# Normalised attention followed by a squared-ReLU network: the last row tile's seven products in another order, its upper rows stored by halves, and the weight pieces converted at other due times

## The chip, the cores and the metric

The kernel runs on one core of a Trainium2 chip. The metric is the device time of one execution in microseconds (us), lower being better. Four executions of the kernel before gave a median of 1434.13 us, from 1432.71 to 1435.56. The profile is of one execution that took 1433.29 us, of which the profiled span is 1431.9 us.

## The reference

There are 8 batches, 12 heads, 448 rows and a head width of 64. Queries and keys are normalised by their root mean square and multiplied by a gain; softmax attention follows; its output, with the heads side by side, is a matrix of 3584 rows by 768. Two matrix products with a squared ReLU between them follow.

```python
q_n, k_n = rmsnorm(q, g_q), rmsnorm(k, g_k)
attn = softmax(q_n @ k_n.T / sqrt(64))
x = (attn @ v).transpose(0, 2, 1, 3).reshape(3584, 768)
h = maximum(x @ w_in, 0.0)          # w_in: 768 x 2048
out = (h * h) @ w_out               # w_out: 2048 x 768
```

All activations are 32-bit floats. The two weight matrices come as 64-bit floats, because the reference multiplies them by a 64-bit scalar; the kernel turns their bits into 32-bit floats itself.

## The kernel before, in words

**Four passes.** The network runs in four passes `ffn(u)`, u = 0 to 3, of two batches each. Both products are done with seven block products P1 to P7 in place of eight, so each matrix is kept as quarters and as sums of quarters: `IN` and `OUT` list the forms of a piece of `w_in` and `w_out` (the tiles `in_sb` and `out_sb`), and `make_x_forms` and `hidden_sum` make the forms of the left factors. The attention of the first two batches stands ahead of pass 0; the attention of later batches is woven into passes 0, 1 and 2. Pass 3 has no attention beside it.

**One block.** A pass has four blocks. In a block, `first_products` (L696) runs twice, seven products of three steps of the inner dimension each (L705); ACT copies four of the product banks to SBUF (L712), DVE adds a bank and a copy to give the hidden values (L725), ACT does the ReLU and the square (L726, L727). Then `second_products` (L743) does the rows left over (L757), and for three row tiles `tt` the seven products of `SECOND_ORDER` (L786). After each product DVE adds the PSUM bank to the accumulator tile (`add_to`, L827; L803 where it subtracts). `upper_acc` holds c11 and c12 as its two halves of 384 columns, `lower_acc` holds c21 and c22. Three PSUM banks play the three roles in turn: role 0 takes P1, P6 and P7 one upon another, role 1 takes P5 and P3, role 2 takes P2 and then P4. So P6 may not start before c11's addition of P1 has read the bank, P4 not before that of P2, P7 not before that of P6.

**The last block of a pass stores.** When a row tile's accumulator is complete, `(tt, 0)` (upper) and `(tt, 1)` (lower) go into `to_store`, and at P2, at P4 and at the end of the block all that wait there are stored, on SP's queue, as whole rows of 768 (L832). In `SECOND_ORDER` P3 completes c12 and P7 completes c21 and c22, so the last store of the kernel is that of the lower rows of tile 2, after P7 and two additions.

**Steps and their cost.** Each generator step ends in a `yield` of a cost: 18 for a product of `first_products`, 15, 15, 5, 5 for the rows left over, 10 for a product of the row tiles. A block's sum is 14 x 18 + 40 + 21 x 10 = 502, a pass's 2008. `run(until)` takes steps until the cost spent reaches a mark; between marks the attention's instructions are emitted (a "visit", every 2008 / 24 = 83.7, and the turning of the next pair's queries or keys halfway between visits). After every step `run` emits one `make_sum` (L942), one `end_join` (L911), whatever conversions are due, and a few of the attention's small tasks. The order of emission is the order on each engine.

**Conversion of the weights.** There are 64 pieces: for each block eight of `w_in` and eight of `w_out`, each 128 x 384 numbers of 64 bits (384 KB). The call `convert()` number n does four things:

- it ends the open join and begins that of piece n-1 (`join_words`, DVE, L900; the end, at the latest one step on, is two more DVE instructions, L920 and L924);
- it asks SP to load piece n+2 (L868, L873); there are three `words` buffers, so this load waits until the join of piece n-1 has ended, and SP's later loads stand behind it;
- it splits piece n on ACT (three activations, L887 to L889), for which that piece must have landed;
- after the fourth piece of a tile, four sums of forms follow, one a step, on DVE and POOL in turn (L946), and a store of the tile to DRAM (L948), from which passes 1 to 3 load the forms again.

The first 17 calls are made while the attention runs alone (`early`). The other 48 are made within pass 0, when the cost spent reaches the next entry of `late`. Before, entry j stands at 502 + 2 + 31.375 (j - 8): sixteen to a block, evenly. The pieces of `w_in` for the next block fall in the second half of a block, those of `w_out` in the first half of the block that uses them.

Of the kernel before, what the change touches and what calls it, by code (L numbers as in the profile page):

```python
# [21 lines left out]
P = 128  # L22
# [201 lines left out]
def program(ctx, tc, rows, v, g, wide, ones, moe_w_in, moe_w_out, out, shift):  # L224

    nc = tc.nc

    B, H, S, D = v.shape
# [5 lines left out]
    HALF = DM // 2  # L234
    REST = S % P
    NT = S // P
    NBLK = 4
# [431 lines left out]

    FIRST_ORDER = ["P1", "P5", "P2", "P6", "P3", "P4", "P7"]  # L670
    SECOND_ORDER = ["P1", "P2", "P5", "P6", "P4", "P3", "P7"]
    COST_IN, COST_OUT = 12 * NK // 2, 10
    COST = NF // 2 * 7 * COST_IN + NBLK * (NT * 7 + 4) * COST_OUT

# [68 lines left out]
    def second_products(u, blk, hid, sums_, accs):  # L743

        flat = [a.rearrange("p t e s -> p t (e s)") for a in hid]
        ns = [u * NF // 2 + 2 * blk + t for t in range(2)]
        w_sb = [out_sb[n] for n in ns]
        s1, s2, s4 = sums_
        for n in range(4):
            hidden_sum(hid, sums_, 1, n)  # L750

        parts = [(0, 0), (1, 0), (0, 1), (1, 1)]
        for some in (parts[:3], parts[3:]):
            for half in range(2):
                ps = roles[half][:, 0:HALF]
                for a, t in some:
                    nc.tensor.matmul(  # L757
                        ps, lhsT=flat[a][:, t, ds(NT * P, P)], rhs=w_sb[t][:, 2 * a + half, :],
                        start=(a, t) == parts[0], stop=(a, t) == parts[-1],
                    )  # L760
                if some[-1] == parts[-1]:
                    add_to(accs[-1][:, ts(half, HALF)], ps, blk == 0)
                yield len(some) * COST_OUT // 2
        turn_roles(2, 1, 0)

        def store_rows(tt, e):
            queues = (nc.sync, nc.scalar if final and (tt, e) == (NT - 1, 1) else nc.sync)
            if tt is None:
                parts = [(2 * u, P * NT, REST), (2 * u + 1, 0, REST)]
            else:  # L770
                parts = [(2 * u + e, REST * e + P * tt, P)]
            store(accs[-1 if tt is None else 2 * tt + e], parts, queues)

        to_store = deque([(None, 0)])
        final = u == B // 2 - 1
        (a11, s3), (a12, a22) = [(a[:, :, LOWER], a[:, :, UPPER]) for a in flat]
        lefts = {"11": a11, "12": a12, "22": a22, "S1": s1, "S2": s2, "S3": s3, "S4": s4}
        for tt in range(NT):
            upper_acc, lower_acc = accs[2 * tt], accs[2 * tt + 1]
            c11, c12 = [upper_acc[:, ts(h, HALF)] for h in range(2)]  # L780
            c21, c22 = [lower_acc[:, ts(h, HALF)] for h in range(2)]
            for name in SECOND_ORDER:
                role, first, left, right = PRODUCTS[name]
                ps = roles[role][:, 0:HALF]
                for t in range(2):
                    nc.tensor.matmul(  # L786
                        ps, lhsT=lefts[left][:, t, ts(tt, P)], rhs=w_sb[t][:, OUT.index(right), :],
                        start=first and t == 0, stop=t == 1,
                        skip_group_check=not first,
                    )  # L790
                if name == "P1":
                    add_to(c11, ps, blk == 0)
                elif name == "P5":
                    add_to(c22, ps, blk == 0)
                elif name == "P2":
                    add_to(c11, ps)
                elif name == "P6":
                    add_to(c12, ps, blk == 0)
                elif name == "P4":
                    if blk == 0:  # L800
                        nc.scalar.mul(c21, ps, -1.0)
                    else:
                        nc.vector.tensor_tensor(out=c21, in0=c21, in1=ps, op=ALU.subtract)  # L803
                elif name == "P3":
                    add_to(c12, ps)
                else:
                    add_to(c21, ps)
                    add_to(c22, ps)
                    to_store.append((tt, 1))
                if name == "P3":  # L810
                    to_store.append((tt, 0))
                if name in ("P2", "P4") and blk == NBLK - 1:
                    while to_store:
                        store_rows(*to_store.popleft())
                yield COST_OUT
            turn_roles(2, 0, 1)
        while to_store and blk == NBLK - 1:
            store_rows(*to_store.popleft())
        for n in ns:
            del out_sb[n]  # L820
            load_out(n + 2)
# [130 lines left out]
    def convert():  # L952
# [13 lines left out]
    block, tile_pieces = COST // NBLK, 4  # L966
    ahead = 4 * tile_pieces
    early = deque(2 + 2.4 * n for n in range(ahead + 1))
    every = block / ahead
    late = deque(  # L970
        block + 2 + every * (n - 2 * tile_pieces) for n in range(len(all_pieces) - ahead)
    )

    load_weights(0)
    load_weights(1)
# [273 lines left out]
```

## Time and profile before

| | |
|---|---|
| median of 4 runs | 1434.13 us |
| profiled execution, its span | 1433.29 us, 1431.9 us |
| PE, DVE, ACT, POOL busy | 1407.1, 659.8, 592.9, 676.5 us |
| attention alone | 0 to 135.7 us |
| pass 0, blocks 0 to 3 | from 135.7, 227.1, 319.7 and 409.1 to 501.2 us |
| last block of pass 3 | 1360.9 to 1424.8 us |

PE is the matrix engine, PEld its weight loads, DVE the vector engine, ACT the scalar engine, POOL the general engine, SP the engine whose queue (SPq) starts nearly all DMAs. In a timeline row come the start and the busy time in us, the engine, the line of the kernel, the operation, what it writes and reads, how many instructions are merged, and in brackets the idle time before it and what ended it. In a row of waits come the waiting engine and line, what it waited for, the total in us, how often, and the longest.

### The profile page before, as it was taken

The numbers are of one execution on the slowest core, as the hardware profiler recorded it, in microseconds if no ns is written. First come the engines' busy times: TensorE is split into PE (matmuls) and PEld (weight loads), VectorE is DVE, ScalarE is ACT, GpSimd is POOL, SyncE is SP. The second block draws the span as 40 slices with busy tenths as digits, with TensorE's granted clock in tenths as the row PEclk, the third lists the DMA queues.
The fourth block names the chain that finished last, engine by engine and source line by source line (L and its number), as shares of the span: only waits on it lengthen the run. The fifth ranks groups of instructions, "written<-read, shape, count | busy, mean of one in ns | idle before, by whom it ended". The sixth has DMA issues, their size and how long they took to land.

```text
span 1431.9 us, 15428 instructions
## 1 busy us (share of the span) xinstructions
PE 1407.1 (98%) x4932; PEld 681.8 (48%) x4932; DVE 659.8 (46%) x1233; ACT 592.9 (41%) x1114; POOL 676.5 (47%) x676
## 2 busy tenths in 40 slices
PE   7999999999999999999999999999999999999997
PEld 3333444444444445445454544445454455555554
DVE  5997366877768523324252452324233241132413
ACT  6874566557555244442425234351432303212130
POOL 5667654746656646446445565464462422011110
PEclk9999999999999999999999999999999999999999
DMA  5765346664676664444435464343622242313122
GB/s 141 194 194 154 66 112 176 167 204 141 197 203 200 193 174 98 150 112 127 117 68 173 113 182 128 98 133 76 180 70 89 94 154 78 116 50 127 38 89 80
DMA packets 309279, 188.12 MB, mean 131 GB/s; under 512 B 265796, under 2 KB 293316, under 8 KB 300996
## 3 DMA queue, kind: packets, MB, share of 16 engines
q1 hardware_dynamic: 308896, 186.97, 44.8%
q8 instruction: 41, 0.67, 0.2%
q14 instruction: 50, 0.41, 0.1%
q10 hardware_dynamic: 292, 0.07, 0.0%
HBM read 144.57 MB, written 42.40 MB: 131 GB/s over the span
## 4 chain that ended last, share of the span: by engine, by line
PE 89%; DVE 4%; SPq 1%; DMA 1%; issue 1%; POOL 1%; ACT 1%; DVEq 0%; POOLq 0%; ACTq 0%
PE bank L705 35%; PE bank L786 29%; PE bank L477 9%; PE bank L397 8%; PE bank L757 5%; PE bank L507 1%; PE bank L516 1%; PE bank L490 1%; DVE acc L827 1%; SPq L157 1%; PE bank L362 0%; DVE out_sb L946 0%; DMA q_rows<-qk 0%; SPq L166 0%; DVE out_sb L924 0%
## 5 line engine op out<-in xcount | busy, mean ns | idle before, releaser
L705 PE MATMUL bank<-xT,in_sb 128*128 128x448 f32 x1344 | 515.4, 542 | 0.0
L705 PEld LDWEIGHTS bank<-xT,in_sb 128*128 128x128 f32 x1344 | 252.4, 190 | 260.4 <-issue 250.7
L827 DVE TENSOR_TENSOR acc<-acc,bank 128x384 f32<-128x384 f32 x324 | 173.7, 549 | 233.0 <-PE bank L786 185.0
L786 PE MATMUL bank<-out_sb,hid 128*128 128x384 f32 x768 | 266.6, 487 | 0.5 <-DVE acc L827 0.5
L725 DVE TENSOR_TENSOR hid<-bank,part 128x448 f32<-128x448 f32 x128 | 76.9, 621 | 329.3 <-PE bank L705 329.0
L405 ACT ACTIVATE wT<-bank,rr 128x448 f32<-128x448 f32 x288 | 161.2, 633 | 121.5 <-PE bank L397 70.5
L786 PE MATMUL bank<-out_sb,sums 128*128 128x384 f32 x576 | 203.8, 490 | 2.7 <-DVE acc L827 2.6
L786 PEld LDWEIGHTS bank<-out_sb,hid 128*128 128x128 f32 x768 | 145.4, 190 | 104.5 <-DVE acc L827 2.4
L202 POOL TENSOR_TENSOR rr<-ms,minus_half 128x8 f32<-128x8 f32 (+1 forms) x96 | 146.4, 1525 | 92.8 <-DVE ms L195 81.8
L741 POOL TENSOR_TENSOR sums<-hid 128x384 f32<-128x384 f32 x32 | 32.3, 1008 | 301.9 <-ACT hid L727 301.9
L397 PE MATMUL bank<-qT,kT 64*128 64x448 f32 (+1 forms) x768 | 164.4, 573 | 1.5 <-DVE qT L370 1.1
L726 ACT ACTIVATE hid<-hid 128x448 f32<-128x448 f32 x128 | 73.3, 572 | 196.8 <-DVE hid L725 196.8
L786 PEld LDWEIGHTS bank<-out_sb,sums 128*128 128x128 f32 x576 | 107.7, 190 | 87.1 <-issue 8.1
L712 ACT COPY part<-bank 128x448 f32<-128x448 f32 x128 | 67.8, 529 | 175.4 <-PE bank L705 175.4
L424 POOL TENSOR_TENSOR sum<-sum,wT 128x448 f32<-128x448 f32 (+1 forms) x96 | 110.4, 1171 | 10.8 <-ACT wT L405 8.1
L397 PEld LDWEIGHTS bank<-qT,kT 64*128 64x128 f32 (+1 forms) x768 | 55.6, 173 | 103.9 <-issue 69.1
L477 PE MATMUL bank<-wT,vt 128*64 128x448 f32 x480 | 102.2, 546 | 0.0
L757 PE MATMUL bank<-out_sb,hid 128*128 128x384 f32 x256 | 85.6, 488 | 0.0
L528 POOL COPY few<-few 32x14 f32<-32x14 f32 x48 | 9.1, 189 | 153.3 <-DVE few L526 151.4
L424 POOL TENSOR_TENSOR sum<-wT 128x448 f32<-128x448 f32 x48 | 57.1, 1209 | 50.4 <-ACT wT L405 50.4
L192 DVE TENSOR_REDUCE ms<-squares 128x8 f32<-128x512 f32 (+1 forms) x68 | 41.8, 614 | 77.0 <-ACT squares L179 77.0
L727 ACT ACTIVATE hid<-hid 128x448 f32<-128x448 f32 x128 | 73.8, 577 | 4.1
(96 smaller groups left out, 1280.4 us busy)
## 6 DMA issues: line engine op xcount, KB each, us to landing
out_sb<-out_forms SPq DMA_DIRECT2D x24, 1536.0 KB, 9.7
in_sb<-in_forms SPq DMA_DIRECT2D x24, 1344.0 KB, 5.9
words<-in_moe_w_in_dram SPq DMA_DIRECT2D x32, 384.0 KB, 3.9
words<-in_moe_w_out_dram SPq DMA_DIRECT2D x32, 384.0 KB, 3.8
out_forms<-out_sb SPq DMA_DIRECT2D x8, 1536.0 KB, 7.1
in_forms<-in_sb SPq DMA_DIRECT2D x8, 1344.0 KB, 5.8
qk<-in_q_dram SPq DMA_DIRECT2D x96, 96.0 KB, 3.3
qk<-in_k_dram SPq DMA_DIRECT2D x96, 96.0 KB, 2.6
```

Source lines behind the costliest of these rows:

```text
L202: self.nc.gpsimd.tensor_tensor(out=self.rr[i][:, x, 0 : self.count(i)], in0=ms, in1=self.minus_half.to_broadcast(list(ms.shape)), op=ALU.pow,)
L397: nc.tensor.matmul(sc[some], lhsT=turned[p, 1][r, keys], rhs=turned[p, 0][r, :], start=True, stop=True,)
L405: nc.scalar.activation(new_weights((i, m), e), sc, AF.Exp, scale=rows.rr[i][:, 1, 2 * m + e : 2 * m + e + 1],)
L424: nc.gpsimd.tensor_tensor(out=sums[i, e][some], in0=left[some], in1=weights[key_of(i, m), e][some], op=ALU.add)
L477: nc.tensor.matmul(values_bank(i)[ds(e * D, D), :], lhsT=lasts[i % 2][mine, e, :] if m == NJ else values[i][:, m, e, :], rhs=weights[key_o ...
L705: nc.tensor.matmul(ps, lhsT=w_sb[:, IN.index(left), c, :], rhs=forms[u, c][right], start=first and c == 0, stop=c == NK - 1, skip_group_ch ...
L725: nc.vector.tensor_tensor(out=dst, in0=left, in1=right, op=op)
L726: nc.scalar.activation(dst, dst, AF.Relu)
L727: nc.scalar.activation(dst, dst, AF.Square)
L757: nc.tensor.matmul(ps, lhsT=flat[a][:, t, ds(NT * P, P)], rhs=w_sb[t][:, 2 * a + half, :], start=(a, t) == parts[0], stop=(a, t) == parts[-1],
L786: nc.tensor.matmul(ps, lhsT=lefts[left][:, t, ts(tt, P)], rhs=w_sb[t][:, OUT.index(right), :], start=first and t == 0, stop=t == 1, skip_g ...
L827: nc.vector.tensor_tensor(out=acc, in0=acc, in1=ps, op=ALU.add)
```

## The change

Two things are changed. First, in the very last row tile of the kernel (`ends`: last pass, last block, last `tt`), the products go in `LAST_ORDER`: P6 before P5, then P7, P4 and last P3. The lower rows are complete after P4 and are stored there. The upper rows are stored as two halves of 384 columns: c11 after P2, c12 after P3. Second, the due times of the 48 later conversions come from `when(n)`: of each sixteen, the eight calls that join `w_in` pieces fall at 0.40 to 0.82 of a block in steps of 0.06, the eight that join `w_out` pieces at 0 to 0.385 of the next block in steps of 0.055 (and 2 units on), where before all sixteen were a sixteenth (0.0625) apart, from 0.5 of a block on.

```diff
+    LAST_ORDER = ["P1", "P2", "P6", "P5", "P7", "P4", "P3"]
...
-            for name in SECOND_ORDER:
+            ends = final and blk == NBLK - 1 and tt == NT - 1
+            for name in LAST_ORDER if ends else SECOND_ORDER:
...
                     add_to(c21, ps)
                     add_to(c22, ps)
+                    if not ends:
+                        to_store.append((tt, 1))
+                if name == "P3" and not ends:
+                    to_store.append((tt, 0))
+                if ends and name == "P4":
                     to_store.append((tt, 1))
-                if name == "P3":
-                    to_store.append((tt, 0))
+                if ends and name in ("P2", "P3"):
+                    half = int(name == "P3")
+                    nc.sync.dma_start(
+                        out[ds(2 * u * S + P * tt, P), ts(half, HALF)], [c11, c12][half]
+                    )
                 if name in ("P2", "P4") and blk == NBLK - 1:
                     while to_store:
                         store_rows(*to_store.popleft())
...
-    every = block / ahead
-    late = deque(
-        block + 2 + every * (n - 2 * tile_pieces) for n in range(len(all_pieces) - ahead)
-    )
+    def when(n):
+        step, n = divmod(n, ahead)
+        if n < ahead // 2:
+            return block * (step + 0.4 + 0.06 * n)
+        return block * (step + 1 + 0.055 * (n - ahead // 2)) + 2
+
+    late = deque(when(n) for n in range(len(all_pieces) - ahead))
```

## The prediction

> **What bounds the kernel now.** I read the engines' totals first, then what PE waited for, then the timelines of PE, DVE and ACT where it waited, then the end of the span.
>
> ```profile
> PE 1407.1 (98%) x4932; PEld 681.8 (48%) x4932; DVE 659.8 (46%) x1233; ACT 592.9 (41%) x1114; POOL 676.5 (47%) x676
> ```
>
> PE is busy for 1407.1 of 1431.9 us, so a change gains only what PE idles, 24.8 us. Some 13 us of that lie in the attention alone, which the change leaves as it is, and 7.1 us behind the last matmul. In pass 0, where the conversions lie, there are only these waits (PE's timeline, blocks 1 and 2):
>
> ```profile
> 264.20 0.97 PE L507 MATMUL bank<-sum,ones 128*64 128x448 f32 x4 [0.84 <-ACT wT L405]
> ...
> 277.68 2.74 PE L786 MATMUL bank<-out_sb,hid 128*128 128x384 f32 x8
> 280.80 1.56 PE L786 MATMUL bank<-out_sb,sums 128*128 128x384 f32 x4 [0.38 <-DVE acc L827]
> 283.62 1.56 PE L786 MATMUL bank<-out_sb,sums 128*128 128x384 f32 x4 [1.26 <-DVE acc L827]
> ...
> 369.85 2.74 PE L786 MATMUL bank<-out_sb,hid 128*128 128x384 f32 x8
> 372.43 1.45 PE L786 MATMUL bank<-out_sb,sums 128*128 128x384 f32 x4
> 374.83 1.56 PE L786 MATMUL bank<-out_sb,sums 128*128 128x384 f32 x4 [0.94 <-DVE acc L827]
> ```
>
> Eight of these matmuls in a row take 2.58 us (277.68 against the next start where nothing waits), 0.3225 each. By this pitch the group at 283.62 should have started at 277.68 + 12 x 0.3225 = 281.55: 2.07 us lost. In block 2 it is 374.83 - (369.85 + 3.87) = 1.11. With 0.97 at 264.2 (0.84 and the usual overlap of 0.13), the conversions' stage loses 4.15 us. That is the whole prize of the second edit.
>
> DVE's timeline shows who is late in block 1: between the first addition of the rows left over and c11's addition, for which P6 waits, stand one sum and a piece's join.
>
> ```profile
> 277.29 0.54 DVE L827 TENSOR_TENSOR acc<-acc,bank 128x384 f32<-128x384 f32 x1
> 277.75 1.46 DVE L946 TENSOR_TENSOR out_sb<-out_sb 128x384 f32<-128x384 f32 x1
> 279.14 1.15 DVE L900 TENSOR_SCALAR in_sb<-words 128x384 uint32<-128x384 uint32 x1
> 280.21 0.54 DVE L827 TENSOR_TENSOR acc<-acc,bank 128x384 f32<-128x384 f32 x1
> 280.67 1.02 DVE L920 SCALAR_TENSOR_TENSOR in_sb<-words,in_sb 128x384 uint32<-128x384 uint32 x1
> 281.83 1.27 DVE L924 CUSTOM_DVE_ANT_0 in_sb<-words,in_sb 128x768 uint16<-128x768 uint16 x1
> 283.02 1.20 DVE L827 TENSOR_TENSOR acc<-acc,bank 128x384 f32<-128x384 f32 x2
> ```
>
> And ACT's timeline shows two waits for a piece that had not landed: the first delayed the exponentials behind the 264.2 wait, the second, more than twice as long, cost PE nothing, because no work that PE needed stood behind it.
>
> ```profile
> 259.28 0.56 ACT L887 ACTIVATE words<-words 128x384 f32<-128x384 f32 x1 [5.38 <-DMA words<-in_moe_w_out_dram]
> ...
> 380.38 0.55 ACT L887 ACTIVATE words<-words 128x384 f32<-128x384 f32 x1 [11.49 <-DMA words<-in_moe_w_in_dram]
> ```
>
> The end of the span: the last matmul ends at 1424.74, two additions end at 1425.80, then the last store is issued.
>
> ```profile
> 1424.08 2.08 SPq L832 DMA_DIRECT2D out_dram<-acc  x2
> 1424.78 1.02 DVE L827 TENSOR_TENSOR acc<-acc,bank 128x384 f32<-128x384 f32 x2 [0.73 <-PE bank L786]
> ```
>
> The DMA view of the same stretch gives the time to landing, in its last column, of the stores of 128 and of 64 whole rows:
>
> ```profile
> out_dram<-acc SPq DMA_DIRECT2D x6, 384.0 KB, 2.8
> out_dram<-acc SPq DMA_DIRECT2D x2, 192.0 KB, 2.7
> ```
>
> **The end, step by step.** The fourteen matmuls stay, so PE ends at the same distance. After P3 there is one addition of 0.55 in place of two in 1.02: 0.47 us less. The last store is 192 KB in place of 384: the medians say 2.7 against 2.8, so 0.1; the nearest other row is the transfer itself, where the DMA view shows up to 380 GB/s, by which 384 KB pass in 1.0 us, so at most 0.5. I take 0.1, since that row is of just such stores. What else the step issues: one more DMA (0.34 us of SP, which is idle there). The lower rows' store leaves about 0.7 us before P3 ends and the last one 0.6 after; they are 1.3 apart, more than the one microsecond of transfer, so I charge nothing; if they overlap wholly the gain falls by 0.5. The c11 store is queued on SP ahead of the two stores of tile 1 and makes these wait for P2's addition, some 3 us; they are 5 us from the end and nobody waits for them. The banks: P6 now starts one product (1.29) behind P1's end, c11's addition takes 0.03 + 0.56; P7 has P5's 1.29 over c12's addition; P4's 1.29 covers P7's two additions of 1.02. No wait of PE. Sum: -0.6, from -1.0 to 0.
>
> [...]
>
> **The due times, step by step.** I laid both lists over the step costs. Block 1 runs from 502 to 1004 units, 754 being where the two first products end. The eight joins of w_out pieces fall at 520, 538, 574, 610, 646, 664, 700, 736 before, at 520, 538, 574, 592, 628, 646, 682, 700 after; the w_in joins at 769, 789, 824, 854, 884, 914, 944, 984 before, at 718, 736, 769, 794, 824, 854, 884, 914 after. Block 2 is the same 502 on. Number of instructions, bytes and sums are unchanged; all that moves is order. (Block 0 had no wait from conversions: its w_in joins go from 267 to 482 to 216 to 412, beside a DVE that is busy 6.9 us of 15.2 between 183.8 and 199; I charge nothing. If that cover fails, it is one lag like block 2's, 1.1.)
>
> Term 1, the P6 wait. At the seam from 754 on, DVE's order was: end of a join, sum, join, end, first addition, sum, join, second addition, end, c11. It becomes: end, sum, join, end, first addition, second addition, join, c11. Before the first addition that is as much as before; between it and c11 only one L900 (0.32 to 1.30 us) stays of 1.46 + 1.15 + 2.35. So c11's addition ends near 277.3 + 0.46 + 0.46 + 1.3 + 0.55, about 280.1, before P6's turn at 281.55. The waits of 2.07 and 1.11 go: -3.2. What is late next is c12 or c21 behind two sums, a join and two ends (to 834 units), but the visit at 844 gives PE 3.4 us of attention just there, as at 286.4 before; I charge 0.5 a block.
>
> Term 2, the wait at 264.2. The split at 664 units waited 5.4 us, as its load stood on SP behind eight requests for queries and keys. Its request needed the join that ended at 628; that end now comes at 610, and the call before that turn of SP's queue. I take the 0.97 as gone.
>
> Term 3, what the earlier calls hold up. On SP, loads of four pieces move ahead of the next pair's turning, keys and queries; each issue is 0.37 us, but the waiting one holds the queue until a join ends (6.8 us at the longest now). Those rows are for later visits; only 0.4 us of PE's waits are on a DMA, before pass 0. On POOL two of the sums come ahead of the four hidden sums (about 1 us each), while POOL still waits for ACT (3.56 us idle before 363.15). On ACT one more split (1.7 us) comes ahead of the hidden values of P7; these ended at 272.9 in block 1 and PE needs them at the thirteenth matmul of the rows left over, 272.42 + 3.9 = 276.3: 3.4 us of cover. Charge 0, up to the second rival's price. Sum of the due times: -3.2 - 1.0 + 2 x 0.5 = -3.2; I take -3.0, leaving 0.2 for the small new order of SP.
>
> [...]
>
> **Sum.** -0.6 - 3.0 = -3.6 against the profiled execution's 1433.29, so 1429.7; the median of the runs is 0.84 above that execution, so 1430.5.
>
> **Rivals.** First, the lag only moves (a wash): DVE has the same work in the same block, and the joins that left the stretch before c11 delay c12 and c21 instead. For it: DVE is busy 15.8 of 17.4 us from 272.4 on. Against it: it idles for 2.58 us right after. Then only the end gains: 1433.5.
>
> Second, slower: a load too late ahead of the hidden values. The calls at 700, 718 and 736 are one step apart, so the split at 736 needs a load whose request waits for the join ended at 718, one step (2.3 us of matmuls) earlier, where landings of w_in pieces took 3.4, 4.1 and 7.5 (least, median, most). ACT then stands before P7's hidden values, and PE behind it. It costs nothing up to a wait of 3.4 us, and then 1 us per us in each of blocks 1 and 2. The gain of 3.6 is gone at a wait of 3.4 + 1.8 = 5.2, about the 5.38 of the row above. At 8.4, between the two rows shown, it is 2 x 5.0 = 10 lost: 1434.1 - 3.6 + 10 = 1440.5. For it: such waits occur. Against it: these requests now come before, not behind, SP's batch of queries and keys.
>
> Third, the halves are not independent: if c12's addition of P6 had to wait for the c11 store to land (2.7 us) before it writes the same tile, P7 would wait 1.5 us, and the end lose 0.9 in place of winning 0.6: 1432.0. Against it: L900 waits only for L887, though L888 and L889 write the other half-words of its tile before it.
>
> **How the numbers follow.** About 0.2%, 2.9 us, is what a measurement of this kernel can tell: below 1431.3 is faster, above 1437.0 slower. The forecast has 0.62; its own range is 1428.4 (all 4.15 and 1.0 gained, and half a microsecond of spread) to 1432.5, and five sixths of it is below 1431.3: 0.52 faster, 0.10 same. The wash has 0.18 and the third rival 0.04, both same. The late load has 0.16, nearly all slower (0.15). So 0.52, 0.33 and 0.15. The range goes from 1428.4 to 1437.0, which leaves the late load out.
>
> **What would show it.** Right: no wait of PE for L827 around 280 and 373, none for L405 at 264, blocks 1 and 2 shorter by 2.5 and 0.6 us, the last store of 192 KB after one addition of 0.55. Wrong: a wait of PE on L727 or L757's weights at the start of the rows left over, with ACT idle for a piece just before; or DVE waits at c12 or c21. It would also be wrong if the steps of block 0, earlier by some 50 units, met the attention's own loads there.

## The result and the profile after

The changed kernel took 1436.39 us (median; 1433.37 to 1440.96) where the kernel before, run beside it, took 1433.43 (1431.27 to 1436.38). The ratio is 1.0021, with a 95% interval from 1.0017 to 1.0026: slower by 0.21%, some 3.0 us, where 3.6 less was forecast. The profiled execution took 1435.15 us, its span 1433.4. Line numbers move by the lines added: L705 is now L706, L725 to L727 are L726 to L728, L757 is L758, L786 is L788, L827 is L837, L887 to L889 are L897 to L899, the joins L900, L920, L924 are L910, L930, L934, and the sums of forms L946 are L956. Of the attention, L397 makes the scores, L405 the exponentials, L477 and L507 the products with the values and with ones, L335 scales the queries, and L179 and L192 square and add for the normalisation; these lines are the same in both kernels.

The totals of the engines alone tell nothing: PE is busy a little less.

```profile
PE 1405.7 (98%) x4932; PEld 681.3 (48%) x4932; DVE 652.1 (45%) x1233; ACT 591.7 (41%) x1114; POOL 672.9 (47%) x676
```

Busy time by stretch tells where the time lies. The stretches are the attention alone, then the four blocks of pass 0, cut where a block's first product starts; behind the colon come the length, and then PE's busy time ahead of the other engines' (block 3 of before starts at 409.06, so 0.07 us of it are counted to block 2 here). First the kernel before:

```profile
0.00:135.70 135.70, 122.47 (x712) 46.85 (x713) 106.56 (x241) 91.97 (x175) 84.59 (x80) 0.99 0.65 176
135.70:227.10 91.40, 91.27 (x308) 42.34 (x304) 47.99 (x89) 49.30 (x97) 56.37 (x48) 1.00 0.44 105
227.10:319.65 92.55, 90.07 (x298) 41.33 (x296) 70.12 (x120) 53.38 (x105) 53.58 (x43) 1.00 0.61 176
319.65:409.13 89.48, 88.41 (x291) 41.00 (x289) 68.62 (x120) 52.32 (x103) 52.49 (x43) 1.00 0.63 181
409.13:501.31 92.18, 91.96 (x310) 42.22 (x309) 60.83 (x103) 43.54 (x83) 59.63 (x50) 1.00 0.64 196
```

And after:

```profile
0.00:134.10 134.10, 119.91 (x712) 45.45 (x712) 106.96 (x241) 91.75 (x175) 84.52 (x80) 1.00 0.66 178
134.10:226.42 92.32, 91.29 (x309) 42.34 (x305) 48.16 (x90) 48.89 (x97) 57.27 (x49) 1.00 0.49 124
226.42:317.74 91.32, 89.52 (x299) 41.12 (x297) 68.33 (x120) 53.16 (x105) 52.64 (x43) 1.00 0.64 179
317.74:410.55 92.81, 89.90 (x291) 41.83 (x289) 67.32 (x120) 51.99 (x103) 51.10 (x43) 0.98 0.61 173
410.55:504.82 94.27, 92.09 (x311) 42.47 (x309) 55.84 (x102) 43.68 (x84) 57.67 (x49) 1.00 0.59 172
```

The attention alone, which the change leaves as it is, is 1.6 us shorter, because the granted clock was lower there in the profile of before (0.99; PE was busy 122.47 us for the same work in 119.91). The blocks of pass 0 went from 365.6 to 370.7 us, by +0.92, -1.23, +3.33 and +2.09. PE's idle time in them (length less busy) went from 0.13, 2.48, 1.07 and 0.22 to 1.03, 1.80, 2.91 and 2.18, 4.0 us more in all. The other 1.1 us is busy time: 1.5 more in block 2, where the clock stands at 0.98, and 0.55 less in block 1. From there to the last matmul both take the same (923.43 and 923.45), and from the last matmul's end to the span's end it is 5.14 after against 7.16.

PE's timeline names the idle times. These are all waits of its matmuls in pass 0, and two groups that did not wait:

```profile
182.25 0.97 PE L397 MATMUL bank<-qT,kT 64*64 64x448 f32 x4 [1.03 <-ACT qT L335]
...
243.11 0.97 PE L397 MATMUL bank<-qT,kT 64*64 64x448 f32 x4 [0.54 <-ACT qT L335]
...
263.54 0.97 PE L507 MATMUL bank<-sum,ones 128*64 128x448 f32 x4
...
279.55 1.56 PE L788 MATMUL bank<-out_sb,hid 128*128 128x384 f32 x4 [1.07 <-DVE acc L837]
...
283.88 1.56 PE L788 MATMUL bank<-out_sb,hid 128*128 128x384 f32 x4 [0.19 <-DVE acc L837]
...
364.55 0.97 PE L397 MATMUL bank<-qT,kT 64*64 64x448 f32 x4 [2.91 <-ACT qT L335]
365.45 7.12 PE L758 MATMUL bank<-out_sb,hid 128*128 128x384 f32 x16
...
427.24 0.97 PE L397 MATMUL bank<-qT,kT 64*64 64x448 f32 x4 [0.55 <-ACT qT L335]
...
449.25 0.97 PE L507 MATMUL bank<-sum,ones 128*64 128x448 f32 x4 [1.50 <-ACT wT L405]
```

Three things are to be seen. The wait at 264 is gone, and in block 2 there is no wait at the seam any more. In block 1 a wait at the seam is left, now of P2 and P4, 1.07 and 0.19. And a kind of wait is new in the matmuls' brackets of pass 0: L397, the scores of attention, waits for queries that ACT scales (L335), four times and 5.0 us in all. With the wait for the exponentials in block 3 (1.50) the brackets come to 7.8 us, against 3.4 before.

The matmuls' brackets do not show all of it: in pass 0 of the kernel before, no row of scores has one. The last four scores of such a visit need the next pair's queries, and the rows of their weight loads (PEld) show that these came late in the kernel before already, by less:

```profile
182.94 0.20 PEld L397 LDWEIGHTS bank<-qT,kT 64*64 64x64 f32 x4 [0.91 <-ACT qT L335]
242.85 0.19 PEld L397 LDWEIGHTS bank<-qT,kT 64*64 64x64 f32 x4 [0.37 <-ACT qT L335]
...
304.88 0.20 PEld L397 LDWEIGHTS bank<-qT,kT 64*64 64x64 f32 x4 [0.70 <-ACT qT L335]
...
363.69 0.19 PEld L397 LDWEIGHTS bank<-qT,kT 64*64 64x64 f32 x4 [0.91 <-ACT qT L335]
424.81 0.20 PEld L397 LDWEIGHTS bank<-qT,kT 64*64 64x64 f32 x4 [0.37 <-ACT qT L335]
```

In the changed kernel the first two and the last two of these rows have 1.81, 1.31, 3.69 and 1.32, and the one between is gone: twelve scores took 2.76 us there before (from 303.02 to the next matmul) and 1.86 after.

Behind the longest of the new waits, the sixteen matmuls of the rows left over took 7.12 us instead of the 5.43 of before. The busy time by stretches of 2 us shows why (the clock is the third number from the end):

```profile
366.00:368.00 2.00, 2.00 (x5) 1.09 (x4) 1.86 (x4) 1.97 (x5) 1.92 (x3) 0.50 1.04 188
368.00:370.00 2.00, 2.00 (x5) 1.12 (x5) 0.39 (x1) 1.68 (x4) 2.00 (x3) 0.67 0.39 82
```

At the end there is now one addition behind the last matmul, and a store of half the rows' width (L819):

```profile
1427.02 0.56 DVE L805 TENSOR_TENSOR acc<-acc,bank 128x384 f32<-128x384 f32 x1 [0.27 <-PE bank L788]
1428.31 0.55 DVE L837 TENSOR_TENSOR acc<-acc,bank 128x384 f32<-128x384 f32 x1 [0.73 <-PE bank L788]
...
1428.89 0.33 SPq L819 DMA_DIRECT2D out_dram<-acc  x1
```

### Where the new wait comes from

In blocks 0 and 2, the visit behind P7 ends with four score matmuls (64 x 64) that need the next pair's scaled queries. ACT scales them behind P7's hidden values, and these wait for DVE's additions of P7. DVE's timeline of after around the 2.91:

```profile
357.09 0.69 DVE L192 TENSOR_REDUCE ms<-squares 128x8 f32<-128x512 f32 x1 [2.23 <-ACT squares L179]
...
358.46 0.52 DVE L956 TENSOR_TENSOR out_sb<-out_sb 128x384 f32<-128x384 f32 x1
358.90 0.55 DVE L930 SCALAR_TENSOR_TENSOR in_sb<-words,in_sb 128x384 uint32<-128x384 uint32 x1
359.48 0.56 DVE L934 CUSTOM_DVE_ANT_0 in_sb<-words,in_sb 128x768 uint16<-128x768 uint16 x1
359.95 1.16 DVE L910 TENSOR_SCALAR in_sb<-words 128x384 uint32<-128x384 uint32 x1
361.04 1.14 DVE L726 TENSOR_TENSOR hid<-bank,part 128x448 f32<-128x448 f32 x2
```

The twelve matmuls that end with P7 ran from 353.36 for 4.78 us, to 358.14. DVE added them at 361.04, 2.90 us later; the wait is 2.91. From DVE's first addition to PE's scores it is 3.51 us (two hidden values of two activations each and the scaling, on ACT); and between P7's end and these scores PE has its own work for 3.50 us (eight of L477, eight of L397). So there is no cover at all: each microsecond by which DVE is late is a microsecond of wait. ACT's part lies ahead of that, in what DVE waited 2.23 us for:

```profile
354.98 0.54 ACT L897 ACTIVATE words<-words 128x384 f32<-128x384 f32 x1
...
356.45 0.61 ACT L179 ACTIVATE squares<-qk 128x512 f32<-128x512 f32 x1
...
359.48 0.56 ACT L897 ACTIVATE words<-words 128x384 f32<-128x384 f32 x1 [2.00 <-DVE in_sb L930]
...
361.68 0.58 ACT L727 ACTIVATE hid<-hid 128x448 f32<-128x448 f32 x1 [0.59 <-DVE hid L726]
```

The split at 354.98 stands ahead of the squares whose sum DVE takes before P7's additions. The chain of waits goes this way: that split, the squares, the reduction, the sum, the end of a join, the start of the next, the additions. The later split, which waited 2.00 us, is not in the chain. In the profile of before the additions stood right behind P7 (ended 360.05), with DVE idle in front of them:

```profile
360.16 1.16 DVE L725 TENSOR_TENSOR hid<-bank,part 128x448 f32<-128x448 f32 x2 [1.49 <-PE bank L705]
...
361.63 3.02 PE L397 MATMUL bank<-qT,kT 64*128 64x448 f32 x12
```

The same difference can be taken in every profile that follows, from the start and length of the twelve matmuls and the start of DVE's addition:

| kernel, block | P7's end | DVE's addition | late by | PE's wait (matmuls' bracket) |
|---|---|---|---|---|
| before, block 2 | 360.05 | 360.16 | 0.11 | none |
| after, block 0 | 177.72 | 178.74 | 1.02 | 1.03 |
| after, block 1 (no such scores there) | 269.23 | 271.67 | 2.44 | none |
| after, block 2 | 358.14 | 361.04 | 2.90 | 2.91 |
| due times alone, block 2 | 360.20 | 363.08 | 2.88 | 2.89 |
| join ended at once, block 0 | 180.45 | 181.62 | 1.17 | 1.18 |
| join ended at once, block 2 | 361.01 | 362.22 | 1.21 | 1.23 |
| six splits out, block 0 | 179.54 | 179.65 | 0.11 | none |
| six splits out, block 2 | 357.66 | 359.07 | 1.41 | 1.43 |
| `w_in` joins from 0.51, block 2 | 358.54 | 358.65 | 0.11 | none |
| the same, `w_out` 0.06 apart, block 2 | 360.44 | 361.20 | 0.76 | 0.78 |

An addition 0.11 us behind P7's end is the least in these profiles, and the kernel before had it. Against that kernel PE therefore loses what goes beyond 0.11: from the starts of the same matmuls, 0.90 us in block 0 and 2.77 in block 2.

### The profile page after: what moved, and what is told of

It is laid out like the page before. It is cut to its first block, busy times and chain, and to the rows that moved or that the text cites. A ratio compares the mean times of both kernels' runs of the same rounds, so it can differ in the third digit from the quotient of the medians.

```text
span 1433.4 us, 15416 instructions
## 1 busy us (share of the span) xinstructions
PE 1405.7 (98%) x4932; PEld 681.3 (48%) x4932; DVE 652.1 (45%) x1233; ACT 591.7 (41%) x1114; POOL 672.9 (47%) x676
## 4 chain that ended last, share of the span: by engine, by line
PE 87%; DVE 4%; ACT 3%; POOL 2%; SPq 1%; issue 1%; DMA 1%; DVEq 0%; POOLq 0%; ACTq 0%
PE bank L706 32%; PE bank L788 29%; PE bank L477 9%; PE bank L397 8%; PE bank L758 6%; PE bank L490 1%; PE bank L516 1%; ACT wT L405 1%; SPq L157 1%; PE bank L507 1%; PE bank L362 0%; DMA words<-in_moe_w_out_dram 0%; DVE acc L837 0%; ACT hid L728 0%; ACT hid L727 0%
## 5 line engine op out<-in xcount | busy, mean ns | idle before, releaser
L706 PE MATMUL bank<-xT,in_sb 128*128 128x448 f32 x1344 | 515.4, 542 | 0.0
L706 PEld LDWEIGHTS bank<-xT,in_sb 128*128 128x128 f32 x1344 | 252.4, 190 | 260.4 <-issue 250.4
L837 DVE TENSOR_TENSOR acc<-acc,bank 128x384 f32<-128x384 f32 x324 | 173.5, 549 | 241.3 <-PE bank L788 194.8
L788 PE MATMUL bank<-out_sb,hid 128*128 128x384 f32 x768 | 266.8, 487 | 1.7 <-DVE acc L837 1.7
L726 DVE TENSOR_TENSOR hid<-bank,part 128x448 f32<-128x448 f32 x128 | 76.8, 621 | 322.3 <-PE bank L706 322.2
L405 ACT ACTIVATE wT<-bank,rr 128x448 f32<-128x448 f32 x288 | 160.8, 632 | 133.3 <-PE bank L397 96.3
L788 PE MATMUL bank<-out_sb,sums 128*128 128x384 f32 x576 | 203.1, 489 | 0.0
L788 PEld LDWEIGHTS bank<-out_sb,hid 128*128 128x128 f32 x768 | 145.3, 190 | 106.4 <-DVE acc L837 4.3
L397 PE MATMUL bank<-qT,kT 64*128 64x448 f32 (+1 forms) x768 | 164.1, 573 | 6.3 <-ACT qT L335 5.0
L727 ACT ACTIVATE hid<-hid 128x448 f32<-128x448 f32 x128 | 73.3, 573 | 205.8 <-DVE hid L726 205.8
L788 PEld LDWEIGHTS bank<-out_sb,sums 128*128 128x128 f32 x576 | 108.1, 190 | 83.0 <-issue 6.8
L397 PEld LDWEIGHTS bank<-qT,kT 64*128 64x128 f32 (+1 forms) x768 | 55.3, 173 | 108.7 <-issue 66.0
L477 PE MATMUL bank<-wT,vt 128*64 128x448 f32 x480 | 102.2, 546 | 0.0
L758 PE MATMUL bank<-out_sb,hid 128*128 128x384 f32 x256 | 87.3, 495 | 0.0
L192 DVE TENSOR_REDUCE ms<-squares 128x8 f32<-128x512 f32 (+1 forms) x68 | 41.8, 614 | 88.0 <-ACT squares L179 88.0
L728 ACT ACTIVATE hid<-hid 128x448 f32<-128x448 f32 x128 | 73.8, 577 | 4.0
```

What stands on the lines that cost most here:

```text
L397: nc.tensor.matmul(sc[some], lhsT=turned[p, 1][r, keys], rhs=turned[p, 0][r, :], start=True, stop=True,)
L405: nc.scalar.activation(new_weights((i, m), e), sc, AF.Exp, scale=rows.rr[i][:, 1, 2 * m + e : 2 * m + e + 1],)
L477: nc.tensor.matmul(values_bank(i)[ds(e * D, D), :], lhsT=lasts[i % 2][mine, e, :] if m == NJ else values[i][:, m, e, :], rhs=weights[key_o ...
L706: nc.tensor.matmul(ps, lhsT=w_sb[:, IN.index(left), c, :], rhs=forms[u, c][right], start=first and c == 0, stop=c == NK - 1, skip_group_ch ...
L726: nc.vector.tensor_tensor(out=dst, in0=left, in1=right, op=op)
L727: nc.scalar.activation(dst, dst, AF.Relu)
```

## The experiments

All ratios are to the kernel before on the same chip, with their 95% interval. They are not the quotients of the medians given and differ from these by up to 0.0007; where microseconds are given with a ratio, they follow from it. Where nothing else is said, an edit is made to the changed kernel.

### The end alone

The new order and the halves stay, the old due times come back.

```diff
-    late = deque(when(n) for n in range(len(all_pieces) - ahead))
+    every = block / ahead
+    late = deque(
+        block + 2 + every * (n - 2 * tile_pieces) for n in range(len(all_pieces) - ahead)
+    )
```

> The last row tile's new order and its stores alone, with the old due times. Main theory (the due times cost, the end gains): 0.6 to 2.0 us below the kernel before, 1431.4 to 1432.8; the profile ends 5 to 6.5 us after the last matmul, against 7.1 before and 5.1 in the changed kernel, and the waits of PE in pass 0 are those of before (2.0 + 0.9 us on DVE's additions, 0.8 on the exponentials). Rival (the end costs, the due times are neutral): some 3 us above, 1436.4.

1432.47 us against 1434.30, ratio 0.9988 (0.9979 to 0.9996), about 1.7 us less, as expected. Pass 0 has the waits of before again (0.62 at 263; 0.38 and 1.25; 0.95). The end gains, and it is not what made the change slower.

### The due times alone

The edit is made to the kernel before: its order and stores at the end stay.

```diff
-    every = block / ahead
-    late = deque(
-        block + 2 + every * (n - 2 * tile_pieces) for n in range(len(all_pieces) - ahead)
-    )
+    def when(n):
+        step, n = divmod(n, ahead)
+        if n < ahead // 2:
+            return block * (step + 0.4 + 0.06 * n)
+        return block * (step + 1 + 0.055 * (n - ahead // 2)) + 2
+
+    late = deque(when(n) for n in range(len(all_pieces) - ahead))
```

> The new due times alone, with the old order and stores at the end. Main theory: 3.6 to 5 us above the kernel before, 1437.0 to 1438.5, with waits of PE for the scaled queries (ACT's multiplication) of some 5 us in pass 0 and the end 7 us after the last matmul. Rival (the end costs): within 1 us of the kernel before.

1437.04 us against 1434.30, ratio 1.0026 (1.0014 to 1.0037), about 3.7 us more. What PE waited for in the whole execution is the list of after (total, times, longest):

```profile
PE bank L397 <- ACT qT L335: 5.0, 4, 2.9
...
PE bank L786 <- DVE acc L827: 1.9, 3, 1.3
PE bank L507 <- ACT wT L405: 1.7, 1, 1.7
```

The whole loss is in the due times. From the first product of pass 0 to that of pass 1 it is 369.22 us here against 365.61 before, 3.6 more, and no slow clock is in it: the sixteen matmuls behind the wait of 2.89 took 5.43 us. With the end alone it is 365.39.

### The `w_in` joins where they were

```diff
-            return block * (step + 0.4 + 0.06 * n)
+            return block * (step + 0.5 + 0.0625 * n) + 2
```

> The changed kernel with the w_in pieces back at their old due times (0.5 of a block on, in steps of 0.0625), the w_out pieces at the new ones. Main theory (the three calls at 700, 718 and 736 units, with splits that ACT must do ahead of the last hidden values and of the scaled queries, are the cause): no wait of PE on ACT's scaled queries in blocks 0 and 2, total waits of PE in pass 0 at most 2 us, 1429.5 to 1432. Rival (the denser w_out joins make DVE late): still above 1435, with waits on DVE's additions.

1435.29 us, ratio 1.0005 (0.9995 to 1.0016). The waits of blocks 0 and 2 for the queries are gone, as expected, so the `w_in` joins make them. But the time was missed, and so was the forecast of at most 2 us of waits: 0.54 at 245 and at 425 stay, and the wait for the exponentials in block 3 is 2.38. The time lies where the rival had it, but not by its cause: DVE's additions make PE wait for only 0.80. The other three belong to the `w_out` joins, as a run below shows. The granted clock was 0.996 or lower in six of these twelve executions and in five of the 35 of the kernel before; how much that adds to the time here is open.

### The `w_in` joins behind the seam

As dense as in the change, nearly (0.05 for 0.06 of a block), but starting behind P7 of the second first product.

```diff
-            return block * (step + 0.4 + 0.06 * n)
+            return block * (step + 0.51 + 0.05 * n)
```

> The changed kernel with the w_in joins at 0.51 to 0.86 of a block, in steps of 0.05: denser than the change has them, but all behind the last hidden values of the block. Main theory: as with the old w_in times, no wait of PE on the scaled queries, 1429.5 to 1432.5. Rival (density is the cause, wherever it lies): above 1435, with DVE's additions as what PE waits for.

1431.25 us, ratio 0.9981 (0.9972 to 0.9990): 2.7 us less than before, and by the ratio the fastest beside one more below. In block 2 DVE comes to P7's additions in time, and the twelve scores run as in the kernel before:

```profile
358.65 1.16 DVE L726 TENSOR_TENSOR hid<-bank,part 128x448 f32<-128x448 f32 x2 [0.78 <-PE bank L706]
...
360.12 3.02 PE L397 MATMUL bank<-qT,kT 64*128 64x448 f32 x12
```

What is left is 0.51 and 0.69 for DVE at the seams, and the waits of the `w_out` joins: 0.55 and 0.54 for queries, of which none was expected, and 1.67. So the place, not the density, was the fault of the `w_in` part.

### The join ended at once

This takes a different thing away: the `words` buffer is given back a step earlier, so the load behind it is asked for earlier.

```diff
         if begun:
             join_words(begun.pop())
+            end_join()
```

> The changed kernel, but each call ends the join that it begins, so the next request for a piece goes out a step earlier. Theory A (the splits at 718 and 736 units wait for pieces requested one step before): ACT's wait ahead of the last hidden values of block 2 (2.0 us at 359.5) goes, and the 2.9 us that PE waits at 361.6 fall below 1; 1433 to 1434.5. Theory B (it is the work of three splits in a row, and DVE's joins behind them, not the landing): PE still waits 2 us or more there, and the time stays within 1 us of the changed kernel, 1435.5 to 1437.5.

1432.59 us against 1432.82, ratio 0.9992 (0.9983 to 1.0002). ACT's wait of 2.00 is gone. In block 2 PE still waits 1.23, in block 0 1.18. DVE shows why:

```profile
361.15 0.56 DVE L930 SCALAR_TENSOR_TENSOR in_sb<-words,in_sb 128x384 uint32<-128x384 uint32 x1
361.75 0.56 DVE L934 CUSTOM_DVE_ANT_0 in_sb<-words,in_sb 128x768 uint16<-128x768 uint16 x1
362.22 1.15 DVE L726 TENSOR_TENSOR hid<-bank,part 128x448 f32<-128x448 f32 x2
```

The theory of the late load wanted less than 1 us left there, that of the splits' and joins' work 2 us or more, and both a longer time: neither holds alone. Nor is the 1.7 us that went a late load's: the reduction (L192) comes 1.58 us ahead of P7's end where it was 1.05, and what follows it up to the additions takes 2.79 us where it took 3.95. There the join's start (L910) took 0.32 instead of 1.16, and the sum (L956) stands behind the additions.

### Six splits left out

ACT's splits of the six pieces that stand around P7 are not run; DVE joins other numbers of the same size in their place.

```diff
+    UNSPLIT = (17, 18, 33, 34, 49, 50)
...
-            high = words[n][:, :, 1]
+            high, by = words[n][:, :, 1], (4, 1)
+            if n in UNSPLIT:
+                high, by = targets[kind, t][:, form - 1].rearrange("p c n -> p (c n)").bitcast(U32), (0, 0)
...
-            split_words(n)
+            if n not in UNSPLIT:
+                split_words(n)
```

(The two instructions that end a join are changed in the same way.)

> The changed kernel without ACT's split of six pieces, two in each of blocks 0, 1 and 2: those of the calls at 718 and 736 units (216 and 234 in block 0). Their joins stay as three DVE instructions of the same sizes, the pieces are still loaded, and the products use other numbers in their place. Theory B: no wait of PE on the scaled queries in blocks 0 and 2 (1.0 and 2.9 us now), block 3 as it is (0.5 and 1.5), 1432 to 1434. A third theory C (DVE's joins ahead of the last hidden values are enough by themselves): the waits stay above half their size, 1435 or more.

1430.85 us against 1432.82, ratio 0.9989 (0.9979 to 0.9998). Block 0's wait is gone, block 2's is 1.43, which is neither of the two outcomes expected for block 2 (the join's start is L913 here):

```profile
355.13 0.69 DVE L192 TENSOR_REDUCE ms<-squares 128x8 f32<-128x512 f32 x1 [0.77 <-ACT squares L179]
...
358.11 1.04 DVE L913 TENSOR_SCALAR in_sb<-in_sb 128x384 uint32<-128x384 uint32 x1
359.07 1.14 DVE L726 TENSOR_TENSOR hid<-bank,part 128x448 f32<-128x448 f32 x2
```

This parts the 2.91 in two. The reduction now comes 2.53 us ahead of P7's end instead of 1.05: 1.48 sooner, and the wait is 1.48 shorter. That much is ACT's split ahead of the squares. The other 1.43 is DVE's own sum, join end and join start, which are still there.

### `w_out` joins as they were, `w_in` joins late

```diff
-            return block * (step + 0.4 + 0.06 * n)
-        return block * (step + 1 + 0.055 * (n - ahead // 2)) + 2
+            return block * (step + 0.51 + 0.05 * n)
+        return block * (step + 1 + 0.0625 * (n - ahead // 2)) + 2
```

> The new end, the w_out joins at their old due times, the w_in joins at 0.51 to 0.86 of a block in steps of 0.05. If the new w_out times cost what the profiles show (0.5 + 0.5 on scaled queries, 1.7 on exponentials in block 3), these waits go, the 0.6 to 0.8 of the old w_out times at 264 us comes back, and the waits on DVE's additions are about those of the kernel with dense late w_in joins (0.5 and 0.7): total waits in pass 0 about 2 us, 1429 to 1431.5. If the gain of the dense late joins came from the w_out times: waits on DVE's additions of 2.5 us, as before, 1431.5 to 1433.

1432.66 us against 1432.82, ratio 0.9994 (0.9985 to 1.0003). No bracket for queries or exponentials is left in the matmuls' rows. But at the seams DVE is late again, in blocks 1 and 2:

```profile
280.70 4.40 PE L788 MATMUL bank<-out_sb,sums 128*128 128x384 f32 x8 [2.04 <-DVE acc L837]
...
373.06 2.85 PE L788 MATMUL bank<-out_sb,sums 128*128 128x384 f32 x8 [1.19 <-DVE acc L837]
```

So the earlier `w_out` times are what relieves the seam, and also what makes the waits of blocks 1 and 3. (The eight matmuls in 4.40 us, for 2.85, are a lower clock again: 0.83 from 280 to 290.)

### Both remedies at once

The `w_in` joins from 0.51, the join ended at once, and the `w_out` joins 0.06 apart.

```diff
+            end_join()
...
-            return block * (step + 0.4 + 0.06 * n)
-        return block * (step + 1 + 0.055 * (n - ahead // 2)) + 2
+            return block * (step + 0.51 + 0.05 * n)
+        return block * (step + 1 + 0.06 * (n - ahead // 2)) + 2
```

> The new end; each join ended in its own call; the w_in joins at 0.51 to 0.86 of a block in steps of 0.05, so that none stands between the block's last products and its seam; the w_out joins in steps of 0.06, so that the fourth falls behind the visit at 592 units in place of before it. Main theory (late pieces and joins ahead of the last hidden values and the scaled queries are the whole cost of the new times): no wait of PE on the scaled queries, none of 1 us or more on the exponentials, some 1 to 2 us on DVE's additions, 1429 to 1430.5, which is 0.2 to 0.3% below the kernel before. If something else of the new times costs, 1431.5 or more.

1432.01 us against 1433.79, ratio 0.9987 (0.9978 to 0.9996). The time expected was missed; it lies in the range given for the case that something else costs. Ending a join at once puts two DVE instructions ahead of additions that PE waits for: 1.78 at 300 and 1.43 at 393, in products of later row tiles. Only 0.33 and 0.19 are left on queries.

### The old due times, the join ended at once

```diff
         if begun:
             join_words(begun.pop())
+            end_join()
...
-    late = deque(when(n) for n in range(len(all_pieces) - ahead))
+    every = block / ahead
+    late = deque(
+        block + 2 + every * (n - 2 * tile_pieces) for n in range(len(all_pieces) - ahead)
+    )
```

> The new end and the old due times, each join ended in its own call. If late requests also cost the kernel before its wait at 264 us: that wait (0.6 to 0.8) goes, the waits on DVE's additions stay within 1 us of their 2.5, 1431 to 1432. If ending a join at once only fills DVE at the wrong place: waits on DVE's additions of 4 us or more, 1433 to 1435.

1432.62 us against 1433.79, ratio 0.9995 (0.9985 to 1.0004), between the two times expected. The earlier request does take the 0.97 at 264 away, but PE waits for DVE six times in pass 0, 6.55 us in all (0.29, 1.58, 1.49, 1.64, 1.34, 0.21).

### `w_out` joins a little later

The `w_in` joins from 0.51 and the `w_out` joins 0.06 of a block apart.

```diff
-            return block * (step + 0.4 + 0.06 * n)
-        return block * (step + 1 + 0.055 * (n - ahead // 2)) + 2
+            return block * (step + 0.51 + 0.05 * n)
+        return block * (step + 1 + 0.06 * (n - ahead // 2)) + 2
```

> The kernel with the w_in joins at 0.51 to 0.86 of a block and the new end, but the w_out joins in steps of 0.06 in place of 0.055, so that the call of the fourth falls behind the visit at 592 units. If the fourth call ahead of that visit is what keeps PE waiting for the scaled queries in blocks 1 and 3 (0.55 and 0.54), both go; the wait of 1.7 on the exponentials in block 3 goes too if its piece is requested ahead of the forms' load again: 1429 to 1431, about 1.5 us below the 0.055 version at equal clock. If those waits only move, 1431 to 1432.5.

1430.88 us against 1432.58, ratio 0.9982 (0.9973 to 0.9991), the same as with 0.055 within the intervals, where about 1.5 us less was expected. The two waits of 0.55 and block 3's on the exponentials are gone, as expected, and others have come: 0.72 and 1.67 for DVE in block 1, 0.78 for the queries in block 2, 0.26 at 392. Pass 0 takes 364.34 us, the least of all profiles, 1.3 less than before.

### The better due times with the old end

The edit is made to the kernel before.

```diff
-    every = block / ahead
-    late = deque(
-        block + 2 + every * (n - 2 * tile_pieces) for n in range(len(all_pieces) - ahead)
-    )
+    def when(n):
+        step, n = divmod(n, ahead)
+        if n < ahead // 2:
+            return block * (step + 0.51 + 0.05 * n)
+        return block * (step + 1 + 0.055 * (n - ahead // 2)) + 2
+
+    late = deque(when(n) for n in range(len(all_pieces) - ahead))
```

> The due times of the kernel with late w_in joins, with the old order and stores at the end. If the two edits add up: the 2.7 us that both gave less the 1.7 of the end alone, so 0.5 to 1.5 us below the kernel before, 1432 to 1433.2; the span ends 6 to 7.2 us after the last matmul, against 5.0 to 6.6 with the new end. If the end brings nothing (its 1.7 us were the clock's lots): 2 to 3 us below, and an end of 5.0 to 5.5 us.

1431.22 us against 1432.58, ratio 0.9990 (0.9981 to 0.9999). With the new end it was 0.9981, and the end alone had 0.9988: that fits two edits that add up, but the intervals overlap. Nor do the profiles show where these due times gain: pass 0 takes 365.26 us here and 365.40 with the new end, against 365.61 before and 365.39 with the end alone. Of the 1.4 us of the ratio, 0.35 is seen there; the rest is open.

## Why the prediction was wrong

**The end** went the forecast way, and of its two parts one held. From the last matmul's end to the last issue it is 1.09 us before and 0.62 after: the 0.47 of the addition. The smaller store gained nothing: the last 192 KB land in 3.0 to 3.5 us in the ten profiles with the new end, 384 KB in 3.0, 3.2 and 3.4 in the three with the old one. The pairs of kernels that differ in the end alone give -1.7, -1.3 and -0.7 us by their ratios, where -0.6 was forecast; only the first is clear of noise, at -3.0 to -0.6. From the last matmul to the span's end it is 5.0 to 6.6 us with the new end and 6.1 to 7.2 with the old one, 5.3 and 6.5 in the mean. What goes beyond the addition lies between landing and the end of the span; whether the edit shortens it, and by what, is open. PE never waits in the last row tile, so the third rival falls.

**Terms 1 and 2** were right in what they take away. By the pitch of 0.3225, block 2 loses nothing at the seam (1.11 before), and the 0.97 at 264 is gone. In block 1 the wait did move, as the allowance for "what is late next" had it, but onto P2 and P4: 279.55 - 277.02 - 1.29 = 1.24 and 283.88 - 280.94 - 2.58 = 0.36, so 1.60 of the 2.07 came back. There "before the first addition that is as much as before" did not hold: that addition began 4.87 us behind the start of the rows left over before, and 7.20 after. Instead of -3.2 and two times 0.5, the seams of blocks 1 and 2 gained 1.4 from start to start. With the `w_out` joins at their old times it is lost again (2.04 and 1.19), which shows that this part of the reasoning held. The first rival, the wash, is the story of block 1 alone.

**Term 3 is the step that failed**: "Charge 0, up to the second rival's price", on a cover of 3.4 us. That cover was read in block 1, against the rows left over. In blocks 0 and 2 another consumer stands ahead of them, the visit's last scores, which need queries that ACT scales behind P7's hidden values. In the profile of before they already stood exactly in time there: they start at 363.69, 3.53 us after DVE's addition at 360.16, and PE's own work lasts 3.50 from P7's end at 360.05. The cover that the moved work met there was 0 and not 3.4. The weight loads' rows of before (0.91 at 182.94 and at 363.69, above) said so; the prediction had read the matmuls' rows alone ("only these waits"). In block 1, where these scores don't stand in that visit, ACT did wait 2.43 us for a piece until 270.75 and DVE's additions came 2.44 late, and it cost nothing, as forecast. The "I charge nothing" for block 0 fell by the same step, at 0.90 (bracket 1.03); that the price in the text, 1.1, came near was luck, since it was taken from block 2's lag at the seam.

Nor was it the second rival's mechanism, a late load in front of the hidden values. Late loads occurred, but the chain goes by DVE: ACT's split ahead of the squares (1.48) and DVE's own sum and joins ahead of the additions (1.43). The prediction counted ACT's moved split only for the hidden values, and DVE's moved joins only for the stretch behind the seam. On DVE they also stand in front of P7's two additions, and that order it never laid out.

Two more prices come from the `w_out` calls, one step earlier now. In blocks 1 and 3 a split stands ahead of the visit's scaling of queries on ACT (0.54 and 0.55 in the brackets, 0.95 each from start to start; gone with the old times and with 0.06). In block 3 the last piece's split has moved ahead of the exponentials. ACT in the kernel before:

```profile
442.03 2.20 ACT L405 ACTIVATE wT<-bank,rr 128x448 f32<-128x448 f32 x4
...
444.93 0.59 ACT L887 ACTIVATE words<-words 128x384 f32<-128x384 f32 x1
```

and after:

```profile
445.42 0.56 ACT L897 ACTIVATE words<-words 128x384 f32<-128x384 f32 x1 [2.32 <-DMA words<-in_moe_w_out_dram]
...
446.91 2.19 ACT L405 ACTIVATE wT<-bank,rr 128x448 f32<-128x448 f32 x4
```

Its load is asked for right behind the 1344 KB of forms that SP loads for pass 1 (SP's queue: 438.30 and 438.95), and the split starts 6.5 us after the request; the piece before it, asked for ahead of those forms in the kernel before (435.86), was split 3.6 us after. That the forms delay it fits this order; no run moves that load alone. That is the second rival's kind of wait, at a place where the prediction had not looked for it: 1.50.

The sum can be taken from the starts of the same matmuls in the profiles of before and after, which leaves nothing out. The late queries cost 0.90, 0.95, 2.77 and 0.95 in blocks 0 to 3, the sixteen slower matmuls 1.70 and the exponentials in block 3 1.58. Against that, 0.92 is gained at 264, 0.36, 1.07 and 0.49 at the seams of blocks 1, 2 and 3, and 0.90 at the twelve scores at 303. That is +5.1, as the blocks show. The last 0.49 and the 0.90 stood in no bracket of a matmul, so the second edit's prize was larger than 4.15. With the end's -2.0 and the attention's -1.6 of this pair of profiles, the spans differ by +1.5.

The medians differ by 3.0. Neither the attention's 1.6 nor the 1.70 of the slower matmuls can be set down to an edit: each is half clock in the one execution profiled (0.66 and 0.50 from 108 to 112 before, where after has 1.00; 0.50 and 0.67 from 366 to 370 after). Without slow clock, the due times alone cost 3.6 in pass 0, and the end gives back 0.47 for the addition, up to 1.1 by the mean of its profiles; that makes 2.5 to 3.1. The clock does not explain the result: at a granted 0.998 the medians are 1436.4 after and 1434.0 before, at 0.999 1435.8 and 1432.1.

## What to carry to other kernels

Before a job is moved to another place on an engine, list everything that stands behind its new place there, on each engine it uses, up to the next thing that the bounding engine consumes, and do so in every block separately: a cover read in one block (3.4 us here) was zero in the next, because another consumer came first. Where cover is zero, the lateness of the first instruction in the chain is the wait, to 0.02 us in the seven rows of the table that have one, so the profile of before can price a move if that start is compared with the bounding engine's own work. Read the rows of the weight loads too, and compare starts: the late queries of the kernel before stood in no matmul's bracket. Of the versions here, the new end with the `w_in` joins behind P7, at 0.51 of a block and then 0.05 apart, has 0.9981 of the time before; that it is faster than the end alone (0.9988) is not shown.

## What the runs showed of the hardware

Idle times of PE of 2.0 to 3.0 us were followed by half the granted clock in some places and not in others. The 2.91 us of after was followed by 0.50 and 0.67 in the rows above, which cost 1.7 us; a wait of 2.89 us at the same place, with the due times alone, was followed by 5.43 us for the same sixteen matmuls, so by none. The shortest that was followed by a slow stretch is the 2.04 at 281 with the `w_out` joins as they were (0.83 from 280 to 290). In the attention alone PE idles 2.38 to 3.03 us around 109 in all thirteen profiles; a slow stretch followed in eight (0.75 to 0.90 from 110 to 120), and in five not (1.00), the 3.03 among them. Idle times of 1.3 to 1.8 us were followed by none (1.00 in the rows of 10 us that hold them). Added up over rows of 2 us, the half clock lasts some 3.4 us (before from 108 on: 0.66, 0.50, 0.99; after from 364 on: 0.98, 0.50, 0.67) or, over rows of 4 us, twice that (with the `w_in` joins where they were, from 108 on: 0.51, 0.63).

The same kernel's time follows the clock granted to the whole run: the changed kernel's medians are 1433.9 us at 1.0, 1435.8 at 0.999, 1436.4 at 0.998, 1437.6 at 0.997 and 1439.1 at 0.996. That clock is a mean, and slow stretches like those above are in it. A change of 0.2% is as much as two thousandths of clock, so single runs of two kernels can't be compared without it.
